# A recurrent attention block and an expanded hidden layer on one core: keys turned on TensorE, the diagonal moved into v, paired operations, and a planner with two-way passes

## Chip, core and metric

The kernel runs on one core of one Trainium2 chip. The metric is the time of one execution on the device in microseconds (us). Below, PE is TensorE, DVE is VectorE, ACT is ScalarE, POOL is GpSimd, and SP is the engine whose queue issues all the transfers. L391 is line 391 of the kernel before.

## What is computed

A linear recurrence with decay (one 48x48 state for each of 4 x 8 batch and head pairs, 768 tokens), and on its output a hidden layer with a leaky slope of its own for each unit:

```python
for t in range(S):                       # S = 768, D = 48
    cur = einsum('bhd,bhe->bhde', u[None] * kt, vt)
    y[:, :, t] = einsum('bhd,bhde->bhe', rt, state + cur)
    state = w[None, :, :, None] * state + einsum('bhd,bhe->bhde', kt, vt)
h = x @ w_in                             # x: 3072 x 384, w_in: 384 x 2048
g = maximum(h, 0) + alpha * minimum(h, 0)
out = g @ w_out                          # w_out: 2048 x 384
```

Everything is fp32.

## The kernel before

**Chunks and pairs.** The 768 tokens are cut into 6 chunks of 128 (`c`), each for 4 batches, so a chunk has 512 columns. The 8 heads go in 4 pairs (`q`), the two heads of a pair in partitions 0 to 47 and 64 to 111. For each pair of a chunk, `attention(c, q, at)` does this. r and k come transposed (112 x 512 each) and are multiplied by tables of powers of the decay, `W[q]` (L299; k takes the table backwards). PE multiplies them to a masked score matrix (`scores`, L339) in two PSUM banks, `A0` and `A1`, one for each head. ACT writes 8 diagonal blocks, ident times `cu` (L346), into `base`; `cu` is the dot product of r, u and k for each token, and chunks 0 and 1 get it from a product on DVE (L307), a small matmul (L314) and a copy (L318), the others on POOL and DVE (L324 to L330). DVE then copies the scores over the strict upper triangle of `base` (L350, one operation for each head). PE multiplies v by `base` and, from chunk 1 on, the state `T[q]` by r, and sums both in the bank `y` (L375 and L380 in chunks 0 and 1, L386 and L391 later). `split` makes a rounded high part `xh` (ACT, L433) and a rest `xl` (DVE, L434) of it, in fp32r, and `lower` moves 16 rows of each to their place by DMA (L269).

**State.** The new state needs k with tokens in the partitions, `kk`, which is loaded by DMA (L288), scaled on DVE by `wtok` (L409), and multiplied with v on PE (`state_product`, L400). `T[q]` is then T times `w128` plus that product (L468 on DVE), or a copy of the product in chunk 0 (L464 on ACT). `wtok` is made once, by `token_table` (L217, L221, L224).

**Hidden layer.** It is made of 96 steps, 16 slices of 128 hidden units for each of 6 chunks. `m_in` (L481) is 9 matmuls of 128x512 into a bank `hp` (two of them); ACT and DVE make g, gh and gl of it (L487 to L492), and `m_out` (L512) is 9 more into three banks `acc0` to `acc2`, a few steps later. The weights of a slice are loaded (`wraw`, 768 KB) and split on ACT and DVE (L245 to L256) ahead of their first step. The order of steps is chunk 0 slices 0 to 8, chunk 1 slices 0 to 8, then the rest of chunk 0, of chunk 1, and chunks 2 to 5.

**Order.** Each operation is a piece with an engine, a cost in us and a rank. `Plan.in_order` simulates the five engines and puts, at each moment, the ready piece with the lowest rank next; the pieces are issued in the order of the starts that come out, so each engine has a fixed order. Buffers in groups with a fixed number of copies are given out in program order. Where the plan has PE idle ahead of the first step, `warm` matmuls (L572) are put in.

**Names of stretches.** The first m_in matmul starts at 33.97 us; up to there is the "fill" (chunk 0's attention). The "mixed stretch", 33.97 to 95.20 us, holds the 9 first steps of chunk 0 (all but the ends of some), chunk 1's attention and the splits of most weights. From 95.20 on chunk 1's and all later steps run, with the later chunks' attention between them.

Of the kernel before, what the change touches and what calls it, by code (L numbers as in the profile page):

```python
# [8 lines left out]
F32 = mybir.dt.float32  # L9
# [21 lines left out]
DMA_RATE = 240.0  # L31
# [22 lines left out]
class Plan:  # L54
# [24 lines left out]
    def in_order(self):  # L79
# [10 lines left out]
        left, heirs = {}, {}  # L90
        number = {p: i for i, p in enumerate(self.pieces)}
        for p in self.pieces:
            p.behind.discard(p)
            need = p.after | p.behind
            left[p] = len(need)
            for q in need:
                heirs.setdefault(q, []).append(p)
        waiting = {e: [] for e in ("PE", "DVE", "ACT", "POOL", "SP")}
        free, dma = dict.fromkeys(waiting, 0.0), 0.0

        def ready(p):
            t = 0.0
            for q in p.after:
                t = max(t, q.end + (0.0 if q.eng == p.eng else 0.2 if q.eng == "PE" else 0.1))
            for q in p.behind:
                t = max(t, q.start + 0.001)
            return t

# [3 lines left out]
        done = []  # L112
        while any(waiting.values()):
            t, e = min((max(free[e], min(x[0] for x in ps)), e) for e, ps in waiting.items() if ps)
            at, p = min((x for x in waiting[e] if x[0] <= t + 0.02), key=lambda x: (x[1].rank, number[x[1]]))
            waiting[e].remove((at, p))
            p.start = max(t, at)
            p.end = free[e] = p.start + p.us
            if e == "SP":
                dma = max(dma, p.end + 1.5) + p.kb / DMA_RATE  # L120
                p.end = dma + 0.3
            done.append(p)
# [4 lines left out]
        assert len(done) == len(self.pieces), "the pieces wait for each other"  # L127
        return sorted(done, key=lambda p: (p.start, number[p]))
# [3 lines left out]
def rwkv_prelu_kernel(ctx: ExitStack, tc, rk, vkr, wP, uP, u, wall, alpha, w, r_all, k_all, v_all, oT):  # L132
# [25 lines left out]
    one, ones, ident = fixed([128, 2], "one"), fixed([128, 128], "ones"), fixed([128, 128], "ident")  # L158
# [4 lines left out]
    W = [fixed([112, L + 1], f"W{m}") for m in range(P)]  # L163
# [8 lines left out]
    bank = pb([128, NT], "acc2")  # L172
# [4 lines left out]
    def load(out, fn, kb, rank, behind=()):  # L177
# [5 lines left out]
    load(utab, lambda: nc.sync.dma_start(utab().rearrange("p h e -> p (h e)"),  # L183
                                         u[None, :].broadcast_to([128, DM])), 196, 19, [wp])
# [19 lines left out]
    def table(m):  # L204
# [4 lines left out]
        add("DVE", 0.55, lambda: nc.vector.reciprocal(t()[:, 0:64], t()[:, 128:64:-1]), w=[t], rank=10 * m - 95)  # L209
        add("DVE", 0.1, lambda: nc.vector.tensor_tensor(  # L210
            out=w128()[:, m:m + 1], in0=t()[:, 128:129], in1=t()[:, 128:129], op=ALU.mult), r=[t], w=[(w128, m)],
            rank=-31)

    def token_table():
        rows, pt = sb([112, P, L], "g", 3), pb([128, P, 2, HI], "A1")
# [57 lines left out]
    def attention(c, q, at):  # L273
# [472 lines left out]
```

## Time and profile before

| | us |
|---|---|
| median of three runs | 528.34 (527.69 to 530.71) |
| the profiled execution, its own time | 530.25 |
| its span, first to last instruction | 528.5 |
| around the span | 1.75 |
| first m_in matmul | 33.97 |
| last matmul ends, about | 521.8 |

Times in rows are us from the start of the span. [...]

### The profile page before, as it was taken

Reading aid. Unit: us, or ns where it says so; the run is one execution under the profiler, and the core shown is the slowest. Engines: PE = TensorE matmul, PEld = TensorE weight load, DVE = VectorE, ACT = ScalarE, POOL = GpSimd, SP = SyncE. Lnnn points to the kernel's source line nnn. Section 1 sums busy time; section 2 is a strip of 40 time slices with the busy share of each in tenths; the row PEclk is TensorE's granted clock in tenths of the full one; section 3 lists DMA queues with packets and bytes.
Section 4 is the critical chain, followed back from the end, with each engine's and each line's share of the span. In section 5 each row is a group of like instructions: output and inputs, shape, how many; then the busy total and the mean of one; then the engine's idle time right before and its main releaser. Section 6 shows DMA issues by size and latency. Waiting matters only on the chain.

```text
span 528.5 us, 8481 instructions
## 1 busy us (share of the span) xinstructions
PE 515.8 (98%) x3310; PEld 409.3 (77%) x3310; DVE 322.5 (61%) x513; ACT 242.5 (46%) x525; POOL 41.3 (8%) x45
## 2 busy tenths in 40 slices
PE   8999899999999999999999999999999999999994
PEld 6877677788887777787787877878777778888883
DVE  7799779889847686756663655664535443333331
ACT  4646655566644454543552544552544333332222
POOL 1000012002000112101120101121000000000000
PEclk9899889999999999999999999999999999999999
DMA  7955546453141552341220240230120000100001
GB/s 225 273 181 182 178 154 211 149 193 122 31 164 31 159 170 64 109 118 45 62 66 17 91 119 30 83 89 2 36 90 1 1 2 1 60 1 0 0 1 64
DMA packets 24877, 47.22 MB, mean 89 GB/s; under 512 B 4096, under 2 KB 12416, under 8 KB 24832
## 3 DMA queue, kind: packets, MB, share of 16 engines
q1 hardware_dynamic: 24832, 46.62, 27.9%
q8 instruction: 28, 0.46, 0.4%
q14 instruction: 17, 0.14, 0.1%
HBM read 37.96 MB, written 6.29 MB: 84 GB/s over the span
## 4 chain that ended last, share of the span: by engine, by line
PE 94%; DVE 2%; ACT 2%; issue 1%; DMA 1%; SPq 0%; ACTq 0%
PE hp L481 38%; PE acc L512 38%; PE A L339 5%; PE y L391 2%; PE y L386 2%; PE y L375 1%; PE A L391 1%; PE y L400 1%; PE y L380 1%; PE acc L314 1%; PE acc L572 1%; PE y L314 1%; ACT base L346 1%; DMA raw<-rk 1%; PE A L400 1%
## 5 line engine op out<-in xcount | busy, mean ns | idle before, releaser
L488 DVE SCALAR_TENSOR_TENSOR g<-hp,alph,g 128x512 f32<-128x512 f32 x96 | 72.0, 750 | 133.6 <-ACT g L487 133.3
L487 ACT ACTIVATE g<-hp 128x512 f32<-128x512 f32 x96 | 57.4, 598 | 161.5 <-PE hp L481 160.6
L481 PE MATMUL hp<-xh,wh 128*128 128x512 f32 x288 | 117.0, 406 | 0.0
L481 PE MATMUL hp<-xh,wl 128*128 128x512 f32 x288 | 114.6, 398 | 0.2 <-DVE wl L256 0.2
L481 PE MATMUL hp<-xl,wh 128*128 128x512 f32 x288 | 114.2, 397 | 0.0
L492 DVE TENSOR_TENSOR gl<-g,gh 128x512 fp32r<-128x512 f32 x96 | 67.9, 707 | 37.9 <-ACT gh L491 36.6
L491 ACT ACTIVATE gh<-g 128x512 fp32r<-128x512 f32 x96 | 60.6, 631 | 60.5 <-DVE g L488 58.3
L512 PE MATMUL acc<-gh,wh 128*128 128x512 f32 x288 | 85.2, 403 | 1.3 <-ACT gh L491 1.3
L512 PE MATMUL acc<-gh,wl 128*128 128x512 f32 x288 | 83.2, 396 | 0.0
L512 PE MATMUL acc<-gl,wh 128*128 128x512 f32 x288 | 83.1, 396 | 0.0
L481 PEld LDWEIGHTS hp<-xh,wh 128*128 128x128 f32 x288 | 54.4, 189 | 13.9 <-issue 0.4
L512 PEld LDWEIGHTS acc<-gh,wh 128*128 128x128 f32 x288 | 52.6, 188 | 15.6 <-ACT gh L491 2.6
L481 PEld LDWEIGHTS hp<-xl,wh 128*128 128x128 f32 x288 | 54.4, 189 | 13.0
L512 PEld LDWEIGHTS acc<-gl,wh 128*128 128x128 f32 x288 | 54.1, 188 | 13.1
L481 PEld LDWEIGHTS hp<-xh,wl 128*128 128x128 f32 x288 | 54.5, 189 | 12.6 <-DVE wl L256 0.6
L512 PEld LDWEIGHTS acc<-gh,wl 128*128 128x128 f32 x288 | 54.0, 188 | 12.8
L346 ACT ACTIVATE base<-ident,cu 128x128 f32<-128x128 f32 x192 | 61.2, 390 | 0.3
L324 POOL TENSOR_TENSOR rr<-rr,kk 128x384 f32<-128x384 f32 x16 | 20.5, 1282 | 314.6 <-DMA kk<-vkr 218.7
L299 DVE TENSOR_TENSOR raw<-raw,W 112x512 f32<-112x512 f32 x46 | 36.3, 809 | 0.6 <-DMA raw<-rk 0.6
L350 DVE COPY_PREDICATED base<-strict,A 128x512 f32<-128x512 uint8 x44 | 30.5, 729 | 2.7 <-PE A L339 2.4
L339 PEld LDWEIGHTS A<-raw 48*128 48x128 f32 x352 | 23.0, 197 | 8.2 <-issue 7.1
L339 PE MATMUL A<-raw 48*128 48x128 f32 x352 | 27.5, 296 | 0.3 <-DVE wtok L224 0.3
(90 smaller groups left out, 423.0 us busy)
## 6 DMA issues: line engine op xcount, KB each, us to landing
wraw<-wall SPq DMA_DIRECT2D x16, 768.0 KB, 4.8
raw<-rk SPq DMA_DIRECT2D x46, 224.0 KB, 3.1
v<-vkr SPq DMA_DIRECT2D x24, 192.0 KB, 4.0
kk<-vkr SPq DMA_DIRECT2D x24, 192.0 KB, 3.5
rr<-vkr SPq DMA_DIRECT2D x16, 192.0 KB, 2.4
oT<-o SPq DMA_DIRECT2D x12, 256.0 KB, 2.0
oT<-g SPq DMA_DIRECT2D x6, 256.0 KB, 2.5
xh<-xh SPq DMA_DIRECT2D x36, 32.0 KB, 2.0
```

The lines of the kernel that those rows point to most:

```text
L299: add("DVE", 0.72, lambda t=t, tab=tab: nc.vector.tensor_tensor(out=t(), in0=t(), in1=tab().broadcast_to([112, B, L]), op=ALU.mult), r=[W[ ...
L324: add("POOL", 1.2, lambda: nc.gpsimd.tensor_tensor(out=rt(), in0=rt(), in1=k(), op=ALU.mult), r=[k] + ([wh[12]] if c == 2 else []), w=[rt] ...
L339: nc.tensor.matmul(A[g]()[:, b], k0()[half(g), b], r()[half(g), b], start=(b == 0), stop=(b == B - 1), skip_group_check=True)
L346: add("ACT", 0.36, lambda g=g, b=b: nc.scalar.activation(base[g]()[:, b], ident(), AF.Copy, scale=cu()[:, g, b:b + 1]), r=[cu, ident], w=[ ...
L350: add("DVE", 0.75, lambda g=g: nc.vector.copy_predicated(base[g](), strict()[:, None, :].broadcast_to([128, B, L]), A[g]()), r=[strict, A[ ...
L391: nc.tensor.matmul(y[g]()[half(o), j * L:(j + 1) * L], v()[:, g * B + b], base[g]()[:, b], start=False, stop=(j == 1), skip_group_check=True)
L481: nc.tensor.matmul(hp(), a[i]()[:, k], x[c]()[:, k], start=(k == 0 and j == 0), stop=(k == NK - 1 and j == 2))
L487: add("ACT", 0.6, lambda: nc.scalar.activation(g(), hp(), AF.Copy), r=[hp], w=[g], rank=n - 100)
L488: add("DVE", 0.75, lambda: nc.vector.scalar_tensor_tensor(out=g(), in0=hp(), scalar=alph()[:, i:i + 1], in1=g(), op0=ALU.mult, op1=ALU.max ...
L491: add("ACT", 0.64, lambda: nc.scalar.activation(gh(), g(), AF.Copy), r=[g], w=[gh], rank=n - 100)
L492: add("DVE", 0.73, lambda: nc.vector.tensor_tensor(out=gl(), in0=g(), in1=gh(), op=ALU.subtract), r=[g, gh], w=[gl], rank=n - 99)
L512: nc.tensor.matmul(banks[k](), a[i]()[:, NK + k], x(), start=(begin and j == 0), stop=(end and j == 2))
```

## The change

Keys: the loads of `kk` in chunks 0 and 1 go. Instead PE transposes the scaled k0 (four 112x128 transposes, `turn_k`) into PSUM, ACT copies it to `k`, and the state is scaled as a whole by `w128` in an ACT copy; in chunk 1 one more matmul adds the old state (`ident` x `T[q]`) to the product in PSUM. `scale_k` stays for chunks 2 to 4, and `token_table` moves behind the fill. Diagonal of chunk 0: `base` is zeroed once (two tiles), and ACT scales v by `cu` (`vc`, 8 operations of 48 columns), which PE adds by 8 more matmuls with `ident`. Pairs: r and k come in one load of 448 KB and one DVE product over both (except pair 3 of chunk 0), for which ACT writes the backward table beside the forward one; the two heads' masks are one DVE operation of 1024 columns over one two-bank tile `A`. `kk` has two copies where it had three; the three `acc` banks are one tile. The table of u loads behind weights 1. The planner: engines may overlap operations (OVERLAP), and 12 rounds of a forward pass, ordered by urgency, and a backward pass that sets the urgency anew; the round with the earliest end is kept.

```diff
-DMA_RATE = 240.0
+DMA_RATE = 270.0
+OVERLAP = {"DVE": 0.08, "ACT": 0.1}
+ROUNDS = 12
...
+        best = None
+        urgency = {p: p.rank for p in self.pieces}
+        for n in range(ROUNDS):
+            order = self.forward(urgency, number)
+            end = max(p.end for p in order)
+            if best is None or end < best[0]:
+                best = end, {p: (p.start, p.end) for p in order}
+            urgency = self.backward(number)
...
+    def run(self, need, ready, key):
...
+        while any(waiting.values()):
             t, e = min((max(free[e], min(x[0] for x in ps)), e) for e, ps in waiting.items() if ps)
-            at, p = min((x for x in waiting[e] if x[0] <= t + 0.02), key=lambda x: (x[1].rank, number[x[1]]))
+            at, p = min((x for x in waiting[e] if x[0] <= t + 0.02), key=lambda x: key(x[1]))
             waiting[e].remove((at, p))
...
+            yield p, max(t, at)
+            free[e] = max(t, at) + p.us - OVERLAP.get(e, 0.0)
...
+    def forward(self, urgency, number):
...
+        for p, start in self.run({p: p.after | p.behind for p in self.pieces}, ready,
+                                 lambda p: (urgency[p], number[p])):
+            p.start, p.end = start, start + p.us
...
+    def backward(self, number):
...
+        was = {p: p.start + p.us for p in self.pieces}
+        for p, at in self.run({p: heirs[p] | followers[p] for p in self.pieces}, ready,
+                              lambda p: (-was[p], -number[p])):
+            ends[p], starts[p] = at, at + p.us
...
+        return {p: -starts[p] for p in self.pieces}
...
-    W = [fixed([112, L + 1], f"W{m}") for m in range(P)]
+    W = [fixed([112, 2 * (L + 1)], f"W{m}") for m in range(P)]
...
+        add("ACT", 0.35, lambda: nc.scalar.activation(t()[:, L + 1:2 * L + 1], t()[:, L - 1::-1], AF.Copy), w=[t],
+            rank=10 * m - 95)
...
+    bases = [sb([128, 2, B, L], "base", 2) for _ in range(2)]
+    for t in bases:
+        add("POOL", 1.0, lambda t=t: nc.gpsimd.memset(t().rearrange("p g b t -> p (g b t)"), 0.0), w=[t], rank=-60)
...
+            load(pair[0], lambda: nc.sync.dma_start(pair[0]().rearrange("p j b t -> p (j b t)"), rk[c, q]), 448,
+                 early + 0.1 * q)
...
+        if c > 1:
             load(k, lambda: nc.sync.dma_start(k().rearrange("p x e -> p (x e)"), vkr[c, q, :, n:2 * n]), 192,
...
+            add("DVE", 1.25, lambda: nc.vector.tensor_tensor(
+                out=pair[0](), in0=pair[0](), in1=tabs().rearrange("p (j t) -> p j t", j=2)[
+                    :, :, None, 0:L].broadcast_to([112, 2, B, L]), op=ALU.mult), r=[tabs], w=pair, rank=rank)
...
+        base = bases[q % 2] if first else sb([128, 2, B, L], "base", 2)
+        vc = sb([128, 2 * B, D], "rr", 2) if first else None
+        for x in range(2 * B if first else 0):
+            add("ACT", 0.25, lambda x=x: nc.scalar.activation(
+                vc()[:, x], v()[:, x], AF.Copy, scale=cu().rearrange("p g b -> p (g b)")[:, x:x + 1]), r=[cu, v],
+                w=[(vc, x)], rank=at - 0.9)
...
+        add("DVE", 1.28, lambda: nc.vector.copy_predicated(
+            base().rearrange("p g b t -> p (g b) t"), strict()[:, None, :].broadcast_to([128, 2 * B, L]),
+            A_of().rearrange("p g b t -> p (g b) t")), r=[strict] + heads, w=[base],
+            rank=10 * q - 76 if first else at - 1.5 if c != 1 else -60)
...
+        if c < 2:
+            kt = pb([128, B, L], "hp", 2) if first else pb([128, 2, B, L], "A")
+            kt_of = (lambda: kt()) if first else (lambda: kt()[:, 1])
+            def turn_k():
+                for b in range(B):
+                    nc.tensor.transpose(kt_of()[:, b, 0:112], k0()[:, b], ident()[0:112, 0:112])
+            late = q - 30 if first else -59
+            add("PE", 0.5, turn_k, r=pair + [ident], w=[kt if first else (kt, 1)], rank=late)
+            add("ACT", 0.55, lambda: nc.scalar.activation(
+                k().rearrange("p (g b) e -> p b g e", g=2), kt_of().rearrange("p b (g e) -> p b g e", g=2)[:, :, :, 0:D],
+                AF.Copy), r=[kt if first else (kt, 1)], w=[k], rank=q - 30 if first else -49)
...
-                U = mine = pb([112, B * D], "A0")
+                U, mine = kt, (kt, 0)
...
-                for b in () if first else range(B):
+                for b in range(B):
                     for g in range(2):
...
+                        a, x = (vc()[:, g * B + b], ident()) if first else (T[q]()[half(g), b], r()[half(g), b])
+                        nc.tensor.matmul(y()[half(g), b], a, x, start=False, stop=(b == B - 1), skip_group_check=True)
...
+            if plain and not first:
+                nc.tensor.matmul(u_rows(slice(0, 112)).rearrange("p b e -> p (b e)"), ident()[0:112, 0:112],
+                                 T[q]().rearrange("p b e -> p (b e)"), start=False, stop=True, skip_group_check=True)
...
+        if plain:
+            add("ACT", 0.4, lambda: nc.scalar.activation(
+                T[q](), u_rows(slice(0, 112)), AF.Copy, scale=w128()[:, q:q + 1]), r=[mine, (w128, q)], w=[T[q]],
+                rank=-48)
...
+    jobs += [(begins[2] - 16, 2, token_table), (9, 2, u_table)]
```

## Rows read from the trace of the kernel before

**Rows 1.** The page, part 1 (busy us, share of the span, instructions) and one line of part 2 (TensorE's granted clock in tenths of full speed, in 40 equal slices of the span, some 13 us each).

```profile
PE 515.8 (98%) x3310; PEld 409.3 (77%) x3310; DVE 322.5 (61%) x513; ACT 242.5 (46%) x525; POOL 41.3 (8%) x45
...
PEclk9899889999999999999999999999999999999999
```

**Rows 2.** Windows of the engines over the stretches: from:to, length, then each engine's busy us (instructions), PEclk, DMA share, GB/s.

```profile
0.00:33.97 33.97, 31.45 (x300) 26.46 (x300) 26.98 (x51) 18.35 (x50) 1.81 (x13) 0.90 0.73 210
33.97:57.00 23.03, 21.53 (x185) 16.36 (x183) 22.30 (x35) 12.58 (x26) 0.00 (x0) 1.00 0.69 230
57.00:71.00 14.00, 12.29 (x90) 9.45 (x90) 11.02 (x18) 6.85 (x16) 0.00 (x0) 0.76 0.38 118
71.00:95.20 24.20, 23.88 (x186) 18.07 (x184) 21.07 (x32) 16.22 (x35) 5.81 (x4) 1.00 0.65 209
95.20:521.80 426.60, 426.60 (x2556) 339.01 (x2555) 241.09 (x380) 187.90 (x399) 33.71 (x28) 1.00 0.20 64
521.80:528.50 6.70, 0.01 (x1) 0.00 (x0) 0.00 (x0) 0.60 (x1) 0.00 (x0) 0.86 0.33 122
```

**Rows 3.** The timeline of the fill: start, us, engine, operation, in brackets the idle time before it and what released it.

```profile
12.76 1.52 SPq L288 DMA_DIRECT2D kk<-vkr  x3
...
16.62 0.73 DVE L350 COPY_PREDICATED base<-strict,acc 128x512 f32<-128x512 uint8 x1 [1.52 <-ACT base L346]
...
18.10 0.90 SPq L232 DMA_DIRECT2D wraw<-wall  x2
...
20.76 0.69 DVE L434 TENSOR_TENSOR xl<-hp,xh 112x512 fp32r<-112x512 f32 x1 [1.61 <-ACT xh L433]
...
26.00 1.28 DVE L299 TENSOR_TENSOR raw<-raw,W 112x512 f32<-112x512 f32 x2
...
29.70 0.96 DVE L249 SCALAR_TENSOR_TENSOR wx<-wraw,wx 128x768 uint32<-128x768 uint32 x1
...
31.68 0.56 DVE L224 COPY wtok<-A 128x384 f32<-128x384 f32 x1
...
32.27 0.56 DVE L409 TENSOR_TENSOR kk<-kk,wtok 128x384 f32<-128x384 f32 x1
...
33.22 0.95 DVE L256 TENSOR_TENSOR wl<-wx,wh 128x768 fp32r<-128x768 f32 x1
...
33.97 0.50 PE L481 MATMUL hp<-xh,wh 128*128 128x512 f32 x1
```

**Rows 4.** The warm matmuls alone (L572), by stretch: length, PE busy (count), PE weight loads busy (count), PEclk, DMA share, GB/s.

```profile
0.00:33.97 33.97, 14.03 (x104) 10.67 (x104) 0.90 0.73 210
```

**Rows 5.** Windows of PE alone: length, PE busy (count), PEclk, DMA share, GB/s.

```profile
11.88:17.60 5.72, 5.69 (x41) 0.50 1.06 276
59.00:62.40 3.40, 1.69 (x20) 1.00 0.77 256
62.40:70.60 8.20, 8.20 (x63) 0.58 0.12 33
```

**Rows 6.** Waits of PE and of DVE in the mixed stretch: who waited for whom, us in total, times, the longest.

```profile
PE y L375 <- DVE base L350: 1.5, 1, 1.5
PE acc L512 <- ACT gh L491: 1.3, 2, 1.0
...
DVE g L488 <- ACT g L487: 3.4, 4, 1.9
DVE T L468 <- PE A L400: 2.7, 3, 1.5
```

**Rows 7.** The timeline of PE: chunk 1's products (first and last of four pairs), the stall before the second, and one state product of chunk 0.

```profile
42.91 0.67 PE L400 MATMUL y<-v,kk 128*64 128x48 f32 x16
...
50.72 1.09 PE L375 MATMUL y<-base,v 128*64 128x128 f32 x16
...
61.39 1.07 PE L375 MATMUL y<-base,v 128*48 128x128 f32 x14 [1.52 <-DVE base L350]
...
87.87 1.42 PE L375 MATMUL y<-base,v 128*64 128x128 f32 x16
```

**Rows 8.** The chain of waits, in order of time (start, us, what): a pair's sums, scores and product in the fill, a transpose of the token table, and one step's m_in later.

```profile
20.08 0.98 PE acc L314 x8
21.06 1.09 PE acc L339 x16
...
22.48 1.02 PE y L375 x15
...
25.67 0.10 PE A L221
...
102.87 2.10 PE hp L481 x9
```

**Rows 9.** Groups by line and form: busy us, mean ns of one.

```profile
L346 ACT ACTIVATE base<-ident,cu 128x128 f32<-128x128 f32 x192 | 61.2, 390 | 0.3
...
L350 DVE COPY_PREDICATED base<-strict,A 128x512 f32<-128x512 uint8 x44 | 30.5, 729 | 2.7 <-PE A L339 2.4 <-ACT base L346 0.2
...
L468 DVE SCALAR_TENSOR_TENSOR T<-T,w,A 112x192 f32<-112x192 f32 x4 | 1.6, 412 | 2.7 <-PE A L400 2.7
...
L464 ACT ACTIVATE T<-y 112x192 f32<-112x192 f32 x4 | 1.3, 321 | 2.4 <-PE y L400 2.4
```

**Rows 10.** The scaling of kk (L409) alone, in the mixed stretch: length, DVE busy (count), PEclk, DMA share, GB/s.

```profile
33.97:95.20 61.23, 3.77 (x7) 0.94 0.61 196
```

More of the change, by code (lines that the diff above doesn't have):

```diff
@@ L93, in in_order @@
             p.behind.discard(p)
-            need = p.after | p.behind
-            left[p] = len(need)
-            for q in need:
+        best = None
[6 more added lines that the diff above has]
+            urgency = self.backward(number)
+        for p, (start, end) in best[1].items():
+            p.start, p.end = start, end
+        return sorted(self.pieces, key=lambda p: (p.start, number[p]))
+    def run(self, need, ready, key):
+        left, heirs = {}, {}
+        for p in self.pieces:
+            left[p] = len(need[p])
+            for q in need[p]:
                 heirs.setdefault(q, []).append(p)
         waiting = {e: [] for e in ("PE", "DVE", "ACT", "POOL", "SP")}
[L99 to L107, printed above, removed]
+        free = dict.fromkeys(waiting, 0.0)
         for p in self.pieces:
@@ L298, in attention @@
-        for j, (t, tab) in enumerate(((r, lambda: W[q]()[:, None, 0:L]), (k0, lambda: W[q]()[:, None, L - 1::-1]))):
-            add("DVE", 0.72, lambda t=t, tab=tab: nc.vector.tensor_tensor(
-                out=t(), in0=t(), in1=tab().broadcast_to([112, B, L]), op=ALU.mult),
-                r=[W[q]], w=[t], rank=10 * q + j - 90 if first else at - 2)
+        if first:
+            first_k.append(pair[-1])
+            first_v.append(v)
+            if q == P - 1:
+                raw_weights(0, -97, [pair[-1]])
+                raw_weights(1, -95, [v])
@@ L338, in scores @@
                 for g in range(2):
-                    nc.tensor.matmul(A[g]()[:, b], k0()[half(g), b], r()[half(g), b], start=(b == 0),
+                    nc.tensor.matmul(A_of()[:, g, b], k0()[half(g), b], r()[half(g), b], start=(b == 0),
                                      stop=(b == B - 1), skip_group_check=True)
-        add("PE", 1.2, scores, r=[r, k0], w=A, rank=10 * q - 90 if first else at)
-        base = [sb([128, B, L], "base", 4) for _ in range(2)]
-        for g in range(2):
+        add("PE", 1.1, scores, r=pair, w=heads, rank=q - 100 if first else at)
@@ L511, in mm @@
             for k in ks:
-                nc.tensor.matmul(banks[k](), a[i]()[:, NK + k], x(), start=(begin and j == 0), stop=(end and j == 2))
+                nc.tensor.matmul(acc()[:, k], a[i]()[:, NK + k], x(), start=(begin and j == 0), stop=(end and j == 2))
         if n == NM - 1:
@@ L527, in m_out @@
                 if i < NF - 1:
[L528 removed]
+                    add("ACT", 0.6, lambda k=k, o=o: nc.scalar.activation(o(), acc()[:, k], AF.Copy), r=[banks[k]],
                         w=[o], rank=n - 90)
```

196 lines of the change are left out of this document (112 added, 84 removed).

## The prediction

> **What bounds the kernel now.** I read the page first, then windows by stage, then the timeline of the stages that are not full, and last who waits for whom there.
>
> The page shows PE busy for 98% of the span [rows 1], which leaves little to win by the look of it. The windows say where. From 95.20 to 521.80 PE is busy for every one of 426.60 us at the full clock [rows 2]. Nothing that shortens DVE, ACT or a load can show there; only matmuls taken out or put in count, or a new stall. The 6.70 us behind the last matmul are the last copy and store, which the change leaves alone. So the change is decided in the first 95 us, in two stages.
>
> The fill ends when the first m_in starts, at 33.97 us [rows 3]. PE looks busy, but 14.03 us of it are warm matmuls, which do no work [rows 4]. DVE is busy for 26.98 us of the 33.97, most of the rest being before its first data arrive and two waits for ACT of 1.5 and 1.6 us. At the end DVE runs without a gap: the split of weights 0 stands around the token table (0.56) and a scaling of kk (0.56), and its last operation, wl at 33.22, lets m_in go [rows 2, 3].
>
> In the mixed stretch, 61.23 us, PE is busy for 21.53 + 12.29 + 23.88 = 57.70 us, so idle for 3.53 us [rows 2]. The middle window has a mean clock of 0.76 where the others have 1.00. [...] DVE is 97% busy in its first 23 us and 89% over all, in an order it cannot leave: in all it waits 3.4 us for ACT's g and 2.7 us for the state product [rows 2, 6].
>
> **The change part by part.**
>
> *Start of the hidden layer.* The token table and the first scaling leave the fill's end: 0.56 + 0.56 = 1.1 us of DVE. The mask no longer waits for ACT's diagonal blocks, which was one wait of 1.5 us [rows 3]. The blocks themselves (8 x 0.39 of ACT for a pair [rows 9]) give way to 8 scalings of 48 columns, which cost no more than that and no less than nothing; they run beside the mask, not ahead of it. Also some 0.78 MB (three kk of 192 KB, the table of u) no longer stands in the queue ahead of weights 0, whose load was issued at 18.10 [rows 3]; at 210 GB/s [rows 2] that is 3.7 us of transfer, but weights 0 are split only from about 27 us on, so I count nothing for it. Against it: the first r and k come as one load of twice the size, so the first scores start some tenths later; the diagonal adds a second product of 1.02 us for each pair [rows 8] and the transposes stand in the banks `hp`, so pair 3's product waits for pair 0's state product and a copy. Both lie in room that warm matmuls fill now: 4 x 1.02 + 16 x 0.10 = 5.7 us of 14.03 [rows 4, 8]. If that cover were gone they would cost up to 5.7. Bounds: no gain below; above, the 2.7 us named and up to 3.8 us more if the planner moves out what DVE does for chunk 1 and weights 1 in the fill, so 6.5. I take 3.0, near the work that surely leaves the end.
>
> *Operations joined.* Two r and k products take 1.28 us back to back [rows 3]. One of 1024 columns is extrapolated from 0.56 for 384 and 0.95 for 768 columns: 0.95 + 256 x 0.39 / 384 = 1.21. The joined mask: 0.73 for 512 columns [rows 9] plus as many again at the same slope, 1.25, against some 1.3 for two. Less than 0.1 us for each pair of operations, 8 pairs before 95 us: 0 to 0.8 us of DVE, mostly where it has room. I count nothing. [...]
>
> *Keys in the mixed stretch.* Seven scalings of kk go, 3.77 us of DVE [rows 10], and four state updates of 0.41 move to ACT at 0.32 [rows 9], which is busy for 58% of that stretch: 3.77 + 1.6 = 5.4 us of DVE's 54.4 [rows 2]. PE gets 16 transposes, 16 x 0.10 = 1.6 us [rows 8], and four matmuls that add the old state: 192 columns, 112 rows and columns. No row shows one. Below lies the sums' matmul with as wide a weight, 0.98 / 4 = 0.25; above, two fp32r matmuls of 512 columns, 2 x 2.10 / 9 = 0.47 [rows 8]; I take the middle, 0.35, so 1.4 (1.0 to 1.9). Of three state products of chunk 0 that ran after the start at about 0.6 each [rows 7], the buffers force one more into the fill: -0.6 (0 to -1.8). The token table's four transposes now lie in the full stretch: +0.4. Together PE's needed work grows by 1.6 + 1.4 - 0.6 + 0.4 = 2.8 us, and all of it counts once DVE no longer sets the pace.
>
> *Stalls and clock.* With 5.4 us less on DVE and one mask where two stood around another operation, I expect half of the 3.53 us of idle time to go, -1.8 (0 to -3.5), and with the stall at 59 us the low clock behind it, -3.4 (0 to -3.4). The new wait: in chunk 1 the products wait for the mask, then four transposes and a copy on ACT. Queued behind that copy on ACT are g and gh of the running step; hp then stays full, and m_in waits. The chain of a pair, from scores to state, is 1.1 + 1.3 + 0.5 + 0.5 + 2.6 + 0.4 + 0.4 and some tenths for handing over, about 7.5 us, against (87.87 - 50.72) / 3 = 12.4 us between pairs [rows 7], so it should lie beside steps.
>
> *Planner.* No row prices it. In the full stretch it cannot win. In the first 95 us it can win no more than the idle time and low clock above; a wrong cost can lose a stall of the kind in rows 7 anywhere. I put it into the chances.
>
> Sum: -3.0 + 2.8 - 1.8 - 3.4 = -5.4 us. The profiled execution went from 530.25 to 524.9; the median of the runs lies 1.9 us lower than it, so 528.34 - 5.4 = 522.9.
>
> **Rivals.**
>
> *The clock falls all the same* (chance 0.2). PE's margin is thin, and one stall like that at 59 us is enough. [...] Then -3.4 falls away: 526.3.
>
> *The start does not move* (0.12): pair 3's product, held by the banks of the transposes, or a slow fill takes the room that the warm matmuls had. For it: the fill's PE work grows by 5.7 us, and a low clock would double what lies in it. Against: 14.03 us of cover. Then -3.0 falls away: 525.9.
>
> *All of it comes* (0.18): the start gains 6, the idle time goes whole, three state products run in the fill: -6 + 1.6 - 3.5 - 3.4 = -11.3, so 517.0.
>
> *Slower* (0.12): chunk 1's turning of k holds up PE. The two banks of `A` hold the scores, then the transposes and the product, and pair q+1's scores wait for them. The turning adds about 1.35 us of transposes, copy and handing over to each pair. Where no step is ready beside it, four times that is 5.4 us of new idle time, the old 3.5 stays, and the clock falls twice, 2 x 3.4. Then -3.0 + 2.8 + 5.4 + 3.4 = +8.6: 536.9. It decides once steps are short at two pairs or more; the spacing of 12.4 us speaks against.
>
> **How the numbers follow.** The forecast has 0.38, and lies between 521 and 525 by its own bounds. Half a per cent, about what a measurement of this kernel can tell from no change, is 2.6 us, so faster means below 525.7 and slower above 531.0. Faster: 0.38 + 0.18 + a quarter of the clock's 0.2 + half of 0.12 = 0.67. Slower: 0.12, and a little of the clock case, 0.13. The rest, 0.2, is no change to tell. For 8 in 10 I leave out the lower half of the best case and the slower case: 517.0 to 529.5.
>
> **What the new profile would show.** The first m_in at about 31 us, without L224 or L409 ahead of it; fewer warm matmuls, by about half of what followed the first 33; no kk load before 60 us; DVE below 85% in the mixed stretch; PE idle under 2.5 us there with a clock of 0.97 or more; from chunk 1's end on, PE full as before. Wrong would be: a clock below 0.95 in a window between start and chunk 1's end (the second case), a first m_in after 33 (the third), waits of PE for the copied k or for T in chunk 1 of over 3 us (the slower case), or any idle time in chunks 2 to 5, where the planner's order would be to blame.

## The result, and the profile of the changed kernel

The changed kernel takes 532.16 us (median of 18 runs, 530.25 to 534.24), the kernel before, run beside it, 528.76 (18 runs, 524.75 to 531.16). The ratio is 1.0067 (95%: 1.0050 to 1.0084): slower by some 3.5 us. The forecast was 522.9, faster, with a range that ended at 529.5. In the table of experiments below, the median of e7_no_diag is that of its ten fast executions; two slow ones (538.54 and 539.42) are left out.

The profiled execution of the changed kernel took 532.34, its span 530.6. The profiled execution of before lay 1.5 above its own median, so the traces show only 530.6 - 528.5 = 2.1 us of the difference. L numbers from here on are the changed kernel's unless an experiment is named.

Page of the changed kernel, parts 1 and 2, as [rows 1]:

```profile
PE 514.2 (97%) x3352; PEld 409.8 (77%) x3352; DVE 314.2 (59%) x454; ACT 244.6 (46%) x541; POOL 43.0 (8%) x47
...
PEclk9699999999999999999999999999999999999998
```

Windows by stretch (length, then PE, PEld, DVE, ACT, POOL busy, PEclk, DMA share, GB/s), as [rows 2]; PEclk is TensorE's granted clock as a share of full speed:

```profile
0.00:36.21 36.21, 30.56 (x330) 26.43 (x330) 23.89 (x39) 18.12 (x56) 4.55 (x15) 0.86 0.68 189
36.21:57.00 20.79, 19.87 (x166) 15.45 (x165) 20.48 (x29) 15.68 (x36) 0.00 (x0) 1.00 0.62 211
57.00:104.00 47.00, 45.90 (x345) 36.77 (x346) 42.48 (x57) 30.24 (x63) 3.53 (x3) 1.00 0.56 180
104.00:112.00 8.00, 6.88 (x40) 5.11 (x39) 7.72 (x11) 4.74 (x8) 2.09 (x2) 1.00 0.83 278
112.00:523.90 411.90, 410.97 (x2477) 326.01 (x2475) 219.68 (x323) 174.96 (x380) 32.83 (x28) 1.00 0.19 56
```

The low clock of before's mixed stretch [rows 5] is gone: 1.00 in every row but the first. But the fill is longer by 2.24 us and has 0.86 where it had 0.90, and PE still idles behind it: 0.92 + 1.10 + 1.12 + 0.93 = 4.1 us by these rows. Of the last row 0.24 lie behind the last matmul, and 0.69 are one wait for ACT ahead of the last three matmuls, where before had none. DVE has 8 us less work in all (314.2 for 322.5), but from the first m_in to 112 us it is fuller than before: 70.7 of 75.8 us, 93%, where before had 70.2 of 78.0 up to 112 us, 90%.

A span can be split into the start of the first m_in, PE's idle time from there to the last matmul, the work that the low clock lost there, the tail behind the last matmul, and what is left, PE's work at full clock (idle time and clock added up over windows of 5 us):

| us | first m_in | PE's work | idle | lost to the clock | tail | span |
|---|---|---|---|---|---|---|
| before | 33.97 | 480.9 | 3.5 | 3.4 | 6.7 | 528.5 |
| changed | 36.21 | 483.6 | 3.8 | 0.0 | 7.0 | 530.6 |
| measured difference | +2.2 | +2.7 | +0.3 | -3.4 | +0.3 | +2.1 |
| forecast | -3.0 | +2.8 | -1.8 | -3.4 | 0 | -5.4 |

By these traces two terms came as forecast, two did not: the start, wrong by 5.2 us, and the idle time, by 2.1.

**The fill.** Its chain of waits (start, us, what):

```profile
3.15 7.51 DMA up<-uP
10.66 0.02 issue
...
11.17 1.08 POOL uw L246
12.24 0.04 issue
12.29 3.57 PE acc L392 x16
```

`up` is a load of under 2 KB that uw, and so the first sums, need. Before, it was the second transfer in SP's queue, and uw began at 3.12. The passes of the new planner gave it a later start, and with it the sixth place, behind `wp`, three loads of 448 KB (r and k) and one of v. It was issued at 3.15 and landed 7.51 us later. PE's timeline shows what hangs on it (in brackets the idle time before):

```profile
7.47 1.16 PE L422 MATMUL A<-raw 48*128 48x128 f32 x16 [0.53 <-DVE raw L374]
9.49 1.16 PE L422 MATMUL acc<-raw 48*128 48x128 f32 x16 [0.85 <-DVE raw L374]
12.29 3.57 PE L392 MATMUL acc<-uw,g 112*128 112x2 f32 x16 [1.64 <-POOL uw L246]
```

PE idles three times in five microseconds (0.53, 0.85 and 1.64 us), and from 11.50 on its clock is 0.52 over 10.70 us. PE alone (length, busy, PEclk, DMA share, GB/s):

```profile
11.50:22.20 10.70, 9.91 (x69) 0.52 0.60 211
22.20:36.21 14.01, 12.82 (x199) 1.00 0.57 155
```

That costs 10.70 x 0.48 = 5.1 us; before lost 33.97 x 0.10 = 3.4 in its fill [rows 2], 2.9 of them in the window of [rows 5]. The difference, 1.7, is most of the start's loss of 2.2, as far as PE sets the fill's length. For most of the fill it does: the warm matmuls alone in the changed kernel's fill (length, PE busy, PEld busy, PEclk, DMA share, GB/s) are

```profile
0.00:8.00 8.00, 5.50 (x33) 4.01 (x33) 1.00 0.78 194
8.00:36.21 28.21, 1.32 (x9) 0.79 (x9) 0.82 0.65 188
```

so behind the first 33, which run ahead of any data, 1.3 us of cover are left where before had 14.03 - 5.18 = 8.85.

These 1.3 us lie near the end of the fill, and there PE is not what the fill waits for. Behind the sums of the last pair the chain goes on over DVE and ACT:

```profile
29.59 1.31 DVE base L437
...
30.92 0.19 ACT cu L396
...
31.13 1.92 ACT rr L429 x8
33.05 0.31 ACT T L573
...
34.01 0.95 PE hp L482 x16
```

The eight scalings of v run behind the mask, and the copy of a state behind them; a state product waits for that copy, and pair 3's product stands behind it. From 29.56 to 33.41 PE is busy for 2.66 of 3.85 us, 1.32 of them with warm matmuls.

**The mixed stretch.** PE's waits from the first m_in on, as [rows 6] (us in total, times, the longest), and then the two longest in PE's timeline:

```profile
PE hp L595 <- DVE g L602: 1.1, 1, 1.1
PE hp L595 <- DMA xh<-xh: 1.1, 1, 1.1
PE acc L622 <- ACT o L649: 0.7, 1, 0.7
PE A L449 <- DVE base L437: 0.5, 1, 0.5
PE hp L595 <- DVE wl L309: 0.5, 1, 0.5
```

```profile
103.63 0.50 PE L595 MATMUL hp<-xh,wh 128*128 128x512 f32 x1 [1.10 <-DMA xh<-xh]
...
107.70 0.50 PE L595 MATMUL hp<-xh,wh 128*128 128x512 f32 x1 [1.12 <-DVE g L602]
```

The long waits of before [rows 6] are gone; the two longest of the new ones stand where chunk 1's attention ends. Its four products start at 47.52, 63.02, 77.83 and 94.04, so (94.04 - 47.52) / 3 = 15.5 us apart where the kernel before had 12.4 [rows 7]. Chunk 1's first steps come late by that, when chunk 0's are used up, which fits the first of the two waits. The second is for a g that DVE made late, behind two weight splits of 1.30 and 1.65 us (0.95 elsewhere), which ran beside POOL products (1.57 us from 102.92 on, 1.60 from 104.57):

```profile
104.00 1.30 DVE L302 SCALAR_TENSOR_TENSOR wx<-wraw,wx 128x768 uint32<-128x768 uint32 x1
...
105.34 1.65 DVE L305 SCALAR_TENSOR_TENSOR wx<-wraw,wx 128x768 uint32<-128x768 uint32 x1
...
106.91 0.74 DVE L602 SCALAR_TENSOR_TENSOR g<-hp,alph,g 128x512 f32<-128x512 f32 x1
```

### The profile page after: what moved, and what is told of

The parts are those of the page before. It is cut to its first block, busy times and chain, and to the rows that moved or that the text cites. A ratio compares the mean times of both kernels' runs of the same rounds, so it can differ in the third digit from the quotient of the medians.

```text
span 530.6 us, 8466 instructions
## 1 busy us (share of the span) xinstructions
PE 514.2 (97%) x3352; PEld 409.8 (77%) x3352; DVE 314.2 (59%) x454; ACT 244.6 (46%) x541; POOL 43.0 (8%) x47
## 4 chain that ended last, share of the span: by engine, by line
PE 90%; DVE 4%; ACT 2%; DMA 1%; issue 1%; SPq 0%; POOL 0%; POOLq 0%
PE hp L595 37%; PE acc L622 37%; PE A L422 4%; PE y L498 2%; PE y L493 2%; DMA up<-uP 1%; PE y L507 1%; PE A L498 1%; PE y L482 1%; PE acc L392 1%; PE y L488 1%; DVE wl L309 1%; DVE wx L305 1%; PE y L392 1%; ACT base L434 1%
## 5 line engine op out<-in xcount | busy, mean ns | idle before, releaser
L434 ACT ACTIVATE base<-ident,cu 128x128 f32<-128x128 f32 x160 | 50.5, 389 | 2.2 <-DVE cu L408 2.1
L402 POOL TENSOR_TENSOR rr<-rr,kk 128x384 f32<-128x384 f32 x16 | 17.8, 1110 | 311.7 <-DMA kk<-vkr 212.0
L374 DVE TENSOR_TENSOR raw<-raw,W 112x1024 f32<-112x1024 f32 x23 | 32.0, 1394 | 1.4 <-DMA raw<-rk 1.4
L437 DVE COPY_PREDICATED base<-strict,A 128x1024 f32<-128x1024 uint8 x22 | 28.9, 1315 | 1.7 <-PE A L422 1.1
```

Of the source, the lines that this page charges most:

```text
L374: add("DVE", 1.25, lambda: nc.vector.tensor_tensor(out=pair[0](), in0=pair[0](), in1=tabs().rearrange("p (j t) -> p j t", j=2)[:, :, None, ...
L402: add("POOL", 1.2, lambda: nc.gpsimd.tensor_tensor(out=rt(), in0=rt(), in1=k(), op=ALU.mult), r=[k] + ([wh[12]] if c == 2 else []), w=[rt] ...
L434: add("ACT", 0.39, lambda g=g, b=b: nc.scalar.activation(base()[:, g, b], ident(), AF.Copy, scale=cu()[:, g, b:b + 1]), r=[cu, ident], w=[ ...
L437: add("DVE", 1.28, lambda: nc.vector.copy_predicated(base().rearrange("p g b t -> p (g b) t"), strict()[:, None, :].broadcast_to([128, 2 * ...
```

## Experiments

All compute the whole reference. e1_small_first, e12_warm_late and e13_warm_first keep the changed kernel's order, e5_passes_first and e14_passes_warm that of e4_passes; in the others the planner makes a new order for the edited kernel, so that a part's price holds what its order did. m_in is the start of the first m_in matmul; idle and clock are PE's idle time behind it and the work lost there at the low clock, as in the table above; they come from one execution of each kernel. The experiments ran in several sessions and on several chips, each beside the kernel before, so between two of them the ratios compare better than the medians. A difference of 0.01 between two ratios is some 5.3 us. Only the medians of e1, e3 and e10 lie within a range that had been expected; the others lie outside each of theirs, so what is read from those was found behind the run.

| run | median | ratio to before (95%) | m_in | idle | clock |
|---|---|---|---|---|---|
| changed kernel | 532.16 | 1.0067 (1.0050 to 1.0084) | 36.21 | 3.8 | 0.0 |
| e1_small_first | 528.59 | 1.0023 (0.9986 to 1.0060) | 32.54 | 3.1 | 1.7 |
| e2_small_late | 534.67 | 1.0153 (1.0108 to 1.0198) | 35.69 | 6.4 | 0.0 |
| e3_ranks | 532.31 | 1.0093 (1.0055 to 1.0132) | 34.41 | 4.3 | 3.4 |
| e4_passes | 522.63 | 0.9921 (0.9890 to 0.9952) | 34.70 | 1.1 | 0.0 |
| e5_passes_first | 524.10 | 0.9911 (0.9873 to 0.9949) | 32.10 | 2.3 | 5.1 |
| e6_no_keys | 525.59 | 0.9949 (0.9929 to 0.9969) | 31.93 | 4.1 | 0.0 |
| e7_no_diag | 532.45 | 1.0074 (1.0042 to 1.0106) | 34.10 | 6.5 | 3.5 |
| e8_no_join | 526.86 | 0.9970 (0.9941 to 0.9998) | 33.24 | 2.2 | 0.0 |
| e9_token_early | 532.82 | 1.0092 (1.0060 to 1.0124) | 35.23 | 3.9 | 2.0 |
| e10_diag_only | 523.80 | 0.9920 (0.9883 to 0.9957) | 35.42 | 2.6 | 0.0 |
| e11_no_join_token | 523.45 | 0.9910 (0.9877 to 0.9943) | 29.88 | 3.9 | 0.0 |
| e12_warm_late | 529.99 | 1.0045 (1.0018 to 1.0072) | 31.74 | 4.4 | 1.7 |
| e13_warm_first | 527.69 | 1.0000 (0.9974 to 1.0027) | 33.44 | 3.7 | 1.7 |
| e14_passes_warm | 525.21 | 0.9929 (0.9901 to 0.9958) | 35.21 | 0.8 | 0.0 |

### The small loads

In the changed kernel's order, `wp` and `up` first, nothing else moved:

```diff
-        return sorted(self.pieces, key=lambda p: (p.start, number[p]))
+        return sorted(self.pieces, key=lambda p: (-1.0 if p.kb == 1 else p.start, number[p]))
```

> The changed kernel, with the two 1.8 KB loads (wp and up) moved to the head of SP's queue and the order on every other engine kept. If the late landing of up (10.66 us, against about 3 us before) is what costs the fill: the sums start right behind the first scores, PE's idle 1.64 us ahead of them goes, the first m_in starts 2 to 4 us sooner than 36.21, and the time falls by 2 to 4 us against the changed kernel, to 528 to 530. If the fill is slow by its order as a whole: less than 0.7 us. If it is slow by the low clock that small matmuls and transposes bring: the clock stays near 0.52 for 10 us, the first m_in stays after 35 us, and the time falls by 1 us at most.

3.6 us by the medians, and the first m_in 3.67 earlier. By the ratios it is 2.3 us (1.0023 and 1.0067, intervals that just overlap). With these two loads first the changed kernel can no longer be told from the kernel before.

The reverse, in the kernel before:

```diff
-    load(wp, lambda: nc.sync.dma_start(wp(), wP), 1, -100)
-    load(up, lambda: nc.sync.dma_start(up(), uP), 1, -99)
+    load(wp, lambda: nc.sync.dma_start(wp(), wP), 1, -98.9)
+    load(up, lambda: nc.sync.dma_start(up(), uP), 1, -98.395)
```

> The kernel before, with wp third and up eighth in SP's queue, behind the large loads of r and k, where the changed kernel has them. If the place of these loads is the cause: the first sums wait for up until about 10 us, and the time rises by 1.5 to 4 us over the kernel before (530 to 533). If the cause is the changed fill itself: within 0.7 us of the kernel before, since its warm matmuls leave room.

1.5% slower than before. The first m_in comes 1.7 us later; the other large thing in its trace is a wait of 3.3 us for gh (L491 of before), which came with a new order, so the late load by itself is priced by the 1.7.

### Late load or low clock

Changed order and late `up` kept, but warm matmuls in the idle places:

```diff
+        turns = [p for p in order if p.eng == "PE"]
+        more = {turns[2]: 6, turns[3]: 14}
...
-            for _ in range(fill.get(p, 0)):
+            for _ in range(fill.get(p, 0) + more.get(p, 0)):
```

> The changed kernel, its order and its late load of up unchanged, with 6 more warm matmuls ahead of pair 1's scores and 14 ahead of the first sums, in the 0.85 and 1.64 us that PE idles there (8.6 to 12.3 us). If the idle time brings the low clock, and the low clock sets the length of the fill: the clock stays at 1.00 from 12 to 22 us, where it was 0.5 (5.0 us lost), the first m_in comes 3 to 5 us sooner than 36.21, and the time falls by 3 to 5 us from 532.2. If the small matmuls and transposes themselves bring the low clock, or DVE and ACT set the fill's length at any clock: the first m_in within 1 us of 36.21, the time within 1.5 us.

PE's timeline at the place of the 1.64 us, and PE's window of the fill:

```profile
9.40 1.16 PE L422 MATMUL acc<-raw 48*128 48x128 f32 x16
10.50 1.70 PE L682 MATMUL acc<-ident 128*128 128x256 bf16 x14
12.11 1.95 PE L392 MATMUL acc<-uw,g 112*128 112x2 f32 x16
```

```profile
0.00:31.74 31.74, 28.86 (x350) 1.00 0.75 216
```

The sums start no sooner (12.11 against 12.29) but take 1.95 us instead of 3.57, and the first m_in comes 4.47 earlier. So the late load costs little by itself; what costs is the clock, 0.52 over 10.70 us of the changed kernel's fill where this one has 1.00, with 1.3 us of cover left behind it. 2.2 of the 4.47 reach the median, 1.2 by the ratios, whose intervals overlap: its mixed stretch has 1.7 us of low clock that the changed kernel's has not, and 0.6 more idle time.

The same for the first experiment's kernel, six warm matmuls ahead of the third pair's scores:

```diff
+        turns = [p for p in order if p.eng == "PE"]
...
+            for _ in range(fill.get(p, 0) + (6 if p is turns[6] else 0)):
```

> The changed kernel with wp and up first (528.6; first m_in at 32.54), with 6 more warm matmuls ahead of the third pair's scores, where PE idles 0.48 us and the clock falls for some 4 us behind it. If the clock in the fill sets the start: no low clock between 13 and 18 us, first m_in 1 to 2.5 us sooner, 526 to 527.6. If not: within 0.7 us of 528.6.

Inconclusive: in its profile, the slowest of its twelve executions (530.62), PE idled for 0.77 and 0.45 us up to 7.5 and 9.2, and the clock fell at 11.5 (0.75 from 11 to 12 us, 0.50 behind), ahead of the matmuls added, which start at 13.35.

### The planner

One round, that is, the ranks as they were written:

```diff
-ROUNDS = 12
+ROUNDS = 1
```

> The changed kernel planned by one forward pass in the order of the ranks, without the backward passes; wp and up are then first in the queue. If the two-way passes are what makes it slow (by the place of small loads or by another order): 1.5 to 5 us faster than the changed kernel, 527 to 531, first m_in before 34.5 us. If the operations of the change make it slow: 531 to 533.

No difference from the changed kernel, though `wp` and `up` are first in this queue; its fill has a clock of 0.85 all the same. A sooner start is eaten by 3.4 us of low clock, so with these operations neither order is good.

The planner alone (the diff's `OVERLAP`, `ROUNDS`, `DMA_RATE`, `in_order`, `run`, `forward` and `backward`) in the kernel before:

> The kernel before with the planner's part of the change alone (two-way passes, overlap, load rate). Its queue has up behind five large loads too. If the passes are the cause: 1.5 to 5 us slower than before (530 to 534). If the other parts are: within 0.7 us of the kernel before.

The best median of all: 5.7 us below the runs of before beside it, 4.2 by the ratio, with `up` late here too (uw began at 7.67) and the fill's clock as in before (0.90). Windows of its mixed stretch:

```profile
34.70:57.00 22.30, 21.49 (x164) 16.76 (x164) 21.77 (x34) 15.37 (x34) 0.00 (x0) 1.00 0.68 237
57.00:97.00 40.00, 39.73 (x316) 31.81 (x313) 39.74 (x58) 23.05 (x46) 7.82 (x4) 1.00 0.60 193
```

This is the row that the prediction lacked: DVE is busy for 39.74 of 40.00 us with all the work of before, and PE for 39.73. So the stalls of before did not follow from DVE's load, but from the order of the work. PE's work behind the start is 478.6 us where before had 480.9; some 1.3 of that are two state products of chunk 0 that now lie in the fill.

That kernel with the two small loads first:

> The kernel before with the planner's part of the change (as in the run with the passes alone, 522.6), and wp and up put at the head of SP's queue. If the small loads cost every plan of the passes what they cost the changed kernel: 2 to 4 us less, 518.5 to 520.5, the first m_in before 33 us. If that cost came only with the changed operations: 522 to 523.

The first m_in comes 2.6 us sooner, but the time is the same (ratios 0.9911 and 0.9921; the median is 1.5 higher). PE's timeline shows where the start is lost again:

```profile
38.34 1.06 PE L441 MATMUL y<-v,kk 128*64 128x48 f32 x16 [1.36 <-DVE kk L450]
```

Behind that the matmuls of the next 10 us take 0.63 us that take 0.39 at full clock, and 5.1 us are lost. A sooner start met a kk that was not ready.

The planner's kernel with twelve more warm matmuls in the fill:

```diff
+        turns = [p for p in order if p.eng == "PE"]
+        more = {turns[1]: 6, turns[4]: 2, turns[5]: 4}
```

> The fastest version so far (the change's planner alone on the kernel before, 522.6 us) with 12 more warm matmuls: 6 ahead of the first pair's scores, 2 and 4 in the gaps behind the second pair's. Order and operations are unchanged. In that version PE idled 0.70 and 0.42 us at 8.3 and 13.5 us and its clock was 0.62 from 12 to 20 us. Theory (the idle time of PE pulls the clock down, and PE at the low clock sets the length of the fill): clock 0.95 or more through the fill, first m_in at 31.5 to 32.5 instead of 34.70, time 519 to 521. Rival A (behind 20 us the fill is set by DVE, whose scaled kk PE waits for at 30.9 us): the clock rises, the first m_in stays within 0.7 of 34.7, time 522 to 523. Rival B (the earlier start meets a late kk, as with the small loads first): first m_in at 32, then a stall of 1.4 us near 38 us with a low clock behind it, 522 to 524.

None of the three. In its profile, the fastest of its five executions, the first idle place, 0.70 us, is closed (PE is busy from 5 to 13 us without a gap), but the added warm matmuls behind the second pair waited for ACT as well, because they write the bank of its sums, and the clock fell behind that place (PE's timeline):

```profile
13.99 1.85 PE L613 MATMUL acc<-ident 128*128 128x256 bf16 x9 [0.60 <-ACT cu L359]
```

The window 14 to 21 us has 0.52. The first m_in moved by +0.5, and the ratio's interval overlaps that of the planner alone.

### The parts

Each is taken back from the first experiment's kernel. Keys: kk is loaded and scaled again, `token_table` runs in the fill, no old-state matmul:

```diff
-            add("PE", 0.5, turn_k, r=pair + [ident], w=[kt if first else (kt, 1)], rank=late)
-            add("ACT", 0.55, lambda: nc.scalar.activation(
...
-            if plain and not first:
-                nc.tensor.matmul(u_rows(slice(0, 112)).rearrange("p b e -> p (b e)"), ident()[0:112, 0:112],
...
+                k_load()
+                add("DVE", 0.56, scale_k, r=[wtok], w=[k], rank=0.5 * q - 1)
```

> The changed kernel with wp and up first (528.6), and with the keys undone: k of chunks 0 and 1 is loaded and scaled on DVE again, T is updated as before, the token table is made in the fill; the diagonal in v and the joined operations stay, and kk keeps two copies. If turning k costs it (2.7 us more PE work, chunk 1's pairs 15.5 us apart instead of 10.8, so that chunk 1's steps wait): 4 to 7 us faster, 521.5 to 524.5, pairs at most 12 us apart. If the diagonal or the joined operations are the cost: 527 to 530.

3.0 us faster without, 3.9 by the ratios. PE's work is 480.6 us instead of 483.3, nearly as much as that; 1.7 less are lost to the clock, and the idle time is 1.0 longer, with DVE busy for 24.99 of 25.07 us behind the start. Chunk 1's products lie 36.6 us from first to last, against 46.5 in the changed kernel. So the turned keys go with the longer spacing, but the idle time did not fall with it: its waits were others (1.4 us for wl, 1.2 for T).

Diagonal back to `base` by ACT:

```diff
-            add("ACT", 0.25, lambda x=x: nc.scalar.activation(
-                vc()[:, x], v()[:, x], AF.Copy, scale=cu().rearrange("p g b -> p (g b)")[:, x:x + 1]), r=[cu, v],
...
-        for g in range(0 if first else 2):
+        for g in range(2):
```

> The changed kernel with wp and up first (528.6), and with the diagonal of chunk 0 written to base by ACT again, with no second product. If the diagonal in v costs the fill, whose PE work it raises by 4 us: the first m_in 1 to 3 us sooner than 32.5, time 525.5 to 527.5. If keys are the cost: within 1 us of 528.6, since warm matmuls made room for the second product.

3.9 us slower without, 2.7 by the ratios, whose intervals overlap: in the profiles, the start 1.6 later, 3.4 more of idle time, 1.8 more of low clock, 1.9 less work for PE.

Loads, products and masks in halves again:

```diff
-        split_rk = first and q == P - 1
+        split_rk = True
...
-        add("DVE", 1.28, lambda: nc.vector.copy_predicated(
...
+        for g in range(2):
+            add("DVE", 0.75, lambda g=g: nc.vector.copy_predicated(
```

> The changed kernel with wp and up first (528.6), and with r and k loaded and multiplied apart and the two heads' masks as two operations again. By the prediction's pricing (under 0.1 us for each pair of operations): within 1 us of 528.6. If one long operation holds up what is behind it on DVE, or the large load delays the first scores: 2 us faster or more. [...]

1.7 us faster without, though DVE has more instructions; 2.8 by the ratios, whose intervals overlap. In the profiles 1.7 us of low clock in the mixed stretch are gone with it.

The token table back in the fill:

```diff
-        rows, pt = sb([112, P, L], "raw", 3), pb([128, 2, P, 2, HI], "A")
-        at = begins[2] - 16
+        rows, pt = sb([112, P, L], "g", 3), pb([128, 2, P, 2, HI], "A")
+        at = -30
```

> The changed kernel with wp and up first (528.6), and the token table made in the fill again, as before the change. If its new place is what stalls PE at the end of chunk 1's attention (the scores of chunk 2 wait 1.17 us for the banks that it holds, behind a joined product of 2.03 us on DVE, and the clock falls behind it, 1.7 us lost): 2 to 3 us faster, 525.5 to 526.6, no stall over 0.7 us between 95 and 110 us. If chunk 1's attention is simply late there because its pairs are 15.5 us apart: another wait takes its place (for xh's loads), and the time stays within 1 us of 528.6.

4.2 us slower, 2.7 of them at the start, where the fill's clock is 0.81. A wait of 1.2 us for wtok went, and one of 2.3 us for the load of xh stands in its place at 102 us: the wait at the end of chunk 1's attention is not the table's.

The diagonal without keys and joins, and halves together with the early table:

> Both the keys and the joined operations undone in the changed kernel with wp and up first; the diagonal in v and the planner stay. If the costs of the parts add up (keys 3.0, joined operations 1.7): 523 to 525. If what each part does hangs on the plan that comes out: 525 to 529. If the diagonal in v helps by what its removal cost (4.7): faster than the kernel before with planner and loads alone (524.1), 519 to 522.

> The changed kernel with wp and up first, the joined operations undone (526.9) and the token table in the fill; the keys and the diagonal stay. If both parts add up: 524 to 525.5. If the stall at the end of chunk 1's attention is the late attention itself: 526 to 528.

523.80 is 4.8 below the first experiment's kernel, about the sum of the two parts taken back (3.0 + 1.7); by the ratios it is 5.4 for 3.9 + 2.8. Against the planner with its small loads first, which differs from it chiefly by the diagonal, it wins nothing (0.9920 and 0.9911). 523.45 comes from the earliest start of all, 29.88 us, with the fill at full clock though it holds all 16 turnings of k and the table's four (PE alone, behind the first warm matmuls):

```profile
8.00:29.88 21.88, 20.84 (x311) 1.00 0.76 225
```

So the medians make a path: before 528.8; planner alone 522.6; its small loads first 524.1; with the diagonal 523.8; with keys and joins 528.6; with the small loads where the plan had put them 532.2. By the ratios the same path is 1, 0.9921, 0.9911, 0.9920, 1.0023, 1.0067. The change holds a gain of 4 to 6 us, the planner's, and loses 8 to 9.5 behind it; the steps clear of their intervals are the planner's and that to keys and joins.

## Why the prediction was wrong

*Start of the hidden layer* (forecast -3.0, measured +2.2): the step that failed. It read DVE's last operations as what sets the fill's end. In before's rows that is so only nearly: the first m_in matmul started at 33.97, ahead of the end of wl (33.22 + 0.95 = 34.17), and what stood ahead of it on PE was chunk 1's scores, held by the token table, and a state product:

```profile
32.29 1.16 PE L339 MATMUL A<-raw 48*128 48x128 f32 x14 [0.27 <-DVE wtok L224]
33.38 0.67 PE L400 MATMUL y<-v,kk 128*64 128x48 f32 x16
```

The prediction also put the planner into the chances as something that no row prices. Two errors lie in the term. The cover was mis-sized: 14.03 us of warm matmuls were taken, but 5.18 of them are the first 33, which no data could replace; of the 8.85 behind them 1.3 are left, so that PE's work set the pace of most of the fill. And the new order of SP's queue was not worked out, though the rows and the prediction had the parts for it: [rows 5] have the clock of before's fill at 0.50 from 11.88 to 17.60, with PE busy for 5.69 of the 5.72 us, and a rival with a chance of 0.12 says that a low clock "would double what lies in it". That rival is what happened, and it went 2.2 us further than "the start does not move", by the extra low clock. Mean clock times length varies less than the start: 30.6 us before, 31.1 changed, 29.3 in e1_small_first, 31.7 in e12_warm_late, 29.9 in e11_no_join_token, and 28.4 to 31.7 over all runs, where the first m_in lies between 29.88 and 36.21. So the low clock accounts for much of the spread, not for all. The 1.1 us taken from DVE's end did not show. Nor did the scalings of v "run beside the mask": for the last pair they ran behind it, 1.92 us in the chain above. Of the signs named, the first m_in after 33 us had been set down for this case, and the warm matmuls behind the first 33 went from 71 to 9, not to half.

*Stalls* (forecast -1.8, measured +0.3): the cause was misread. DVE's load, 89% of the stretch, was taken for a bound. It was to fall below 85%; the planner filled the room, in part with splits of weights (41.5 us of DVE between the start and 112 us for 38.1), 93%, and the idle time stayed. In e4_passes it rose to 99% (61.5 of 62.3 us in the two rows above), and the idle time went. Of the new stalls the first fits the price that the slower rival named, the turning of k in chunk 1, but by a longer spacing of the pairs (15.5 us against 12.4), not by steps short at each pair; that rival's sum, 536.9, was too high. The second lies in DVE's order, and in e6_no_keys, without the turning, PE idled as long (4.1 us), so that keys cause the stalls is not shown.

*Clock in the mixed stretch* (-3.4): as forecast in the traces, where before has 8.20 us at 0.58 [rows 5], 8.20 x 0.42 = 3.4, and the changed kernel 1.00; and with the cause named, since the wait for the second mask, 1.52 of the 1.71 us that PE idled from 59.00 to 62.40 [rows 5, 7], is gone. That it came is luck in part. The profiled execution of before had a mean clock of 0.985, as low as any of the 110 executions of before that ran beside the experiments; their median is 0.989, so a middling one lost some 0.004 x 528 = 2.1 us less (an estimate), and less was there to win. And every experiment that has both keys and joins (e1, e3, e7, e9, e12, e13) lost 1.7 to 3.5 us to the clock again. Of the eight that lack one or both only e5_passes_first lost any, 5.1, and it has the operations of e4_passes, which lost none. So the gain hangs on an order; that the operations bear on it is not excluded.

*PE's work* (+2.8): +2.7, though by other terms. The old-state matmuls were mis-sized: taken at 0.35 each and bounded by 0.47, they show, in the chain of waits,

```profile
50.21 0.51 PE A L510 x2
```

that is 0.51 for one matmul, which has two records, so 0.6 more for the four. Against that two of chunk 0's three state products moved into the fill, not one, which gives 0.6 back. That keys cost PE's time and give DVE's was right, and "all of it counts" too; what was wrong was that DVE's time was worth something in exchange.

*Operations joined* (nothing): durations as priced, DVE's groups by form up to 95 us:

```profile
L374 DVE TENSOR_TENSOR raw<-raw,W 112x1024 f32<-112x1024 f32 x8 | 9.6, 1215 | 0.8 <-DMA raw<-rk 0.8
L437 DVE COPY_PREDICATED base<-strict,A 128x1024 f32<-128x1024 uint8 x6 | 7.9, 1310 | 0.5 <-PE y L482 0.5
```

1.21 and 1.31 against the 1.21 and 1.25 taken. That undoing the joins would come out 1.7 us faster was not in the forecast; whether the operations or their order cost that is not shown.

*Diagonal*: its price hangs on the rest. Taken out of the kernel with keys and joins it cost 3.9 us (e7_no_diag); put into the planner's kernel it won nothing (e10_diag_only, whose expectation of 519 to 522 for such a gain was missed). The prediction saw one wait of 1.5 us in it. Its ACT operations took 0.32 us each, for 0.39.

What stays open is what decides whether a fill keeps its clock. Idle places of 1.64 us (the changed kernel) and of 0.48 to 0.85 (0.48 in e1_small_first) stood ahead of falls; but in the kernel before it fell at 11.2 (0.54 from there to 11.5), with PE idle for 0.62 us up to 7.28 and then busy for 3.10 of the 3.20 us from 8.00 on; in e8_no_join PE idled for only 0.28 us, up to 12.3 (the change's `cu` from ACT), and it fell at 13.9 (0.58 from 14.5 to 17.8), and in e11_no_join_token, with nearly the same list of matmuls and the same 0.28 us up to 12.0, it did not fall at all (1.00 from 8.00 to 29.88). Nor is it the small loads alone: with them first, the fills of e3, e7, e9 and e10 still have 0.81 to 0.86. Whether the added warm matmuls of e12_warm_late kept the clock by closing the idle places or by what they are, the runs do not separate. The runs show what a low clock costs the fill (5.1 us of the changed kernel's), not a rule for avoiding it. Open too is how much of a part's price is its operations and how much the new order that its plan brought.

## What to carry to other kernels

When a change comes with a new scheduler, try the scheduler alone first, and read the order of the first transfers before anything else: a load of under 2 KB, four places later in a queue, cost 2.3 to 3.6 us here, with PE idle for 1.64 us and a clock of 0.52 over 10.70 us at its place. An engine that is 90% or even 99% busy is not the bound as long as the engine behind it does not wait (DVE in e4_passes: 39.74 of 40.00 us, with PE busy for 39.73); move work between engines only when a row shows the wait that will go, and count the work on the engine that receives it in full where that engine is full. Cover must be counted behind the point where data arrive; and before a longer stage is put down to its waits, its length times its clock should be compared.

## What the runs showed of the hardware

- A transfer of under 2 KB issued behind 448 KB loads in the same queue took 7.51 us to land (3.15 to 10.66); issued second in the queue, in before, its consumer began 1.8 us after the issue (1.29 to 3.12).
- One fp32 matmul of 192 columns with 112 rows took 0.51 us in two records, where the clock was 1.00 (50.00 to 51.00 us of the changed kernel).
- Transposes between other matmuls can stand at the full clock: e11_no_join_token's fill, with 20 of them, has 1.00; that of e9_token_early, with 19, has 0.81. What transposes alone do, no run here shows.
- The product of 1024 columns took 1.22 us in the median of its 23 records. Five took 1.94 to 2.04, each beside a POOL product of L404; one at 355.72 us, beside a POOL product of L402, took 1.22. One of the five in the timeline of all engines:

```profile
175.55 1.38 POOL L404 TENSOR_TENSOR rr<-rr,utab 128x384 f32<-128x384 f32 x1
...
175.98 2.03 DVE L374 TENSOR_TENSOR raw<-raw,W 112x1024 f32<-112x1024 f32 x1
```

- Single executions of one kernel differ by several us together with their mean clock: the kernel before ran from 523.39 (0.999) to 530.82 (0.986) beside e4_passes, so one profile shows one draw of the low clock, and medians decide.
